# First MLP layer of row blocks 2 and 3 in one pass with seven block products for eight on four fifths of its contraction

## Chip, cores and metric

The kernel runs on one core of one Trainium2 chip. The metric is the device time of one execution in microseconds (us). The time before the change is the median of three runs.

## What is computed

`x` has 2048 rows of 640 numbers. After a layernorm, the output is the sum of the input, a two-sided Fourier transform and a two-layer MLP with a hidden width of 1536:

```python
xn = _layernorm(x, axis=-1)
a = jnp.einsum("bsd,ed->bse", xn, dft_hid_re)
b = jnp.einsum("bsd,ed->bse", xn, dft_hid_im)
y = jnp.einsum("ts,bse->bte", dft_seq_re, a) - jnp.einsum("ts,bse->bte", dft_seq_im, b)
h = _gelu(jnp.einsum("bsd,df->bsf", xn, w1) + b1)
out = x + y + jnp.einsum("bsf,fd->bsd", h, w2) + b2
```

Here x is (1, 2048, 640), w1 is (640, 1536) and w2 is (1536, 640), all in float32. The change concerns the first MLP layer, the product of `xn` and `w1`.

## The kernel before

Every matrix product runs in three matmuls: each operand is split into a high part in a short format (`fp32r`) and a low part that holds the rest. ScalarE (ACT) copies the high part, VectorE (DVE) subtracts to get the low part (`split`, L153 to L160), and `product` (L268 to L273) issues high by high, high by low and low by high into one PSUM bank. The names used below: a *form* or *piece* is a split operand of a matmul; a *unit* is one block of 128 of the 1536 hidden columns for one block of 512 rows.

The MLP runs first, over four row blocks t = 0 to 3 of 512 rows, and the Fourier part after it. A counter g runs over 48 units, g = 12 t + i. `hidden(g)` (L279) is the first layer of one unit: five 128-wide chunks of the contraction (640 = 5 x 128), three matmuls each, into one of three banks. `gelu(g)` (L294) applies bias and GELU on ACT, then splits the result into `hs`, of which there are three buffers. `output(g)` (L306) is the second layer of the unit: five blocks of 128 output columns, three matmuls each, into five banks that hold their sums over the twelve units of a row block. In each pass of the main loop (L724) PE does `hidden(g + 2)` and then `output(g)`; ACT and DVE work two units ahead of the second layer. After a row block `add_block` (L323) adds the bias on ACT, transposes on DVE and adds to a tile `xo` on GpSimd (POOL), and three DMAs store that tile to DRAM (`ys`, L750).

All engines execute their instructions in the order in which the program lists them, and nearly all DMAs are issued by the SP queue, in program order too. The order is written out by hand (`manual_schedule`). What stands beside the matmuls:

- In row block 0: the splits of the weights w1 and w2 of the coming units (`prep_w1`, `prep_w2`, with three raw buffers each, `w1r` and `w2r`). They stay in the chip's memory (SBUF) for all four row blocks, in places (`xab`, `xc`, `as`, `r01`, `rt2`) that the Fourier part uses later.
- In row blocks 0 to 2, for the next row block (`background`, L660): loads of `x`, statistics (`ln_stats`), scale (`ln_scale`, whose square root needs another ACT table than GELU), `ln_apply`, which normalises on DVE and stores the rows to a DRAM tensor `xs` in sixteen DMAs, and `load_z`, which reads them back in another layout. `transpose_z` on DVE and `prep_xt` make the split operands of the next row block, mostly in the pass i = 9.
- In row blocks 1 and 2: fifteen steps of `prep_w` (L374), which load, transpose (`turn_w`), combine and split the hidden-side Fourier matrices into the buffer `wst` (two slots, `put_w`, L359), from which ACT issues the stores to DRAM (`wit`, L370).
- A region called `zo` holds one tile at a time: `xp`, then `z` and `xo` by turns.

Of the kernel before, what the change touches and what calls it, by code (L numbers as in the profile page):

```python
# [25 lines left out]
def kernel(  # L26
# [37 lines left out]

    nc = tc.nc
# [22 lines left out]
    xs = dram.tile([NS, P, D], F32, name="xs")  # L88

# [15 lines left out]
    def bank(k):  # L105
# [40 lines left out]
    def row_tile(name):  # L146
        return rows.tile([P, D], F32, tag="row", bufs=4, name=name)
# [25 lines left out]
    xt = {}  # L173

    def load_x(c, eng=nc.sync):
        xt[c] = row_tile(f"x{c}")
        eng.dma_start(xt[c], x[c * P : (c + 1) * P])

    def ln_stats(c):
        m = MV  # L180
        st = ST[c % 2]
        half = D // 2
        for h in range(2):
            nc.vector.bn_stats(st[:, h, :], xt[c][:, h * half : (h + 1) * half])  # L184
        nc.vector.bn_aggr(m[:, c % 4, 0:2], st.rearrange("p a b -> p (a b)"))  # L185

    def ln_scale(c0, n):

        m = MV[:, c0 % 4 : c0 % 4 + n]
# [8 lines left out]
    def ln_apply(c, eng=nc.vector):  # L198
        m = MV[:, c % 4]
# [3 lines left out]

    def ln_apply_chunked(dst, c):

        m = MV[:, c % 4]
# [13 lines left out]
    def new_xt(t, j):  # L220
        XT[j] = mr.tile([P, 2, TB], F32R, tag="xt", bufs=ND, name=f"xt{t}_{j}")

    def load_z(t):
        z = out_pool.tile([P, NB, DQ], F32, tag="zo", bufs=1, name=f"z{t}")
        Z["z"] = z
        for q in range(Q):
            v = xs[:, t * B : (t + 1) * B, q * DQ : (q + 1) * DQ].rearrange("n r d -> r n d")
            nc.sync.dma_start(z[q * B : (q + 1) * B], v)

    def transpose_z(t, j):  # L230
        zt[j] = mr.tile([P, TB], F32, tag="zt", bufs=2, name=f"zt{t}_{j}")
        nc.vector.transpose(
            zt[j].rearrange("p (n i) -> p n i", i=B), Z["z"][:, :, j * B : (j + 1) * B]
        )

    def prep_xt(t, j):
        new_xt(t, j)
        split(XT[j][:, 0], XT[j][:, 1], zt.pop(j))
# [3 lines left out]
    def load_w1(i, eng=nc.sync):  # L242
        if i >= NF:
            return
# [3 lines left out]
        for q in range(Q):  # L248
            eng.dma_start(t[q * B : (q + 1) * B], v[q, :, :, i * P : (i + 1) * P])
# [8 lines left out]
    def prep_w1(i):  # L258
        if i < NF:
            W1[i] = slots[1, i]  # L260
            split(W1[i][:, 0], W1[i][:, 1], w1r.pop(i).rearrange("p a b -> p (a b)"))
# [17 lines left out]
    def hidden(g):  # L279
        i = g % NF  # L280
        acc = bank(g % 3)
# [12 lines left out]
    def gelu(g, acc, fill=lambda k: None):  # L294

        i = g % NF
        a = mr.tile([P, TB], F32, tag="ab", bufs=2, name=f"ab{g}")
        nc.scalar.activation(a, acc, AF.Gelu_apprx_tanh, bias=b1c[:, i : i + 1])  # L298
        fill(0)
# [6 lines left out]
    def output(g):  # L306
        t, i = divmod(g, NF)
        if i == 0:
            oacc[t] = [bank(3 + e) for e in range(ND)]
        hs = HT[g]  # L310
        for e in range(ND):
# [5 lines left out]
    def load_xo(t):  # L317

        xo[t] = out_pool.tile([P, NB, DQ], F32, tag="zo", bufs=1, name=f"xo{t}")
# [15 lines left out]
    def load_w(m, j):  # L335

        t = A["w"].tile([P, EB, B], F32, tag=f"wraw{m}", bufs=1, name=f"wraw{m}_{j}")
# [6 lines left out]
    def turn_w(m, j):  # L344
        t = A["w"].tile([P, D], F32, tag=f"wt{m}", bufs=1, name=f"wt{m}_{j}")
# [13 lines left out]
    def put_w(w, j, main, odd=None, negative=False):  # L359

        n = GWIDE[w] * P
        t = A["w"].tile([P, 2, 3 * P], F32R, tag="wst", bufs=2, name=f"wst{w}_{j}")
# [7 lines left out]
        stores.append(lambda: nc.scalar.dma_start(wits[w][j], t[:, :, :n].bitcast(F32)))  # L370
        if len(stores) == 2:
            put_away()

    def prep_w(s):  # L374
# [29 lines left out]
        put_away()  # L404
# [117 lines left out]
    def load_xr(k):  # L522
# [7 lines left out]
        for half in range(2):  # L530
# [3 lines left out]
            else:  # L534
                r = row_tile(f"xr{k}_{half}")
# [68 lines left out]
    wacc = bank(0)  # L604
# [10 lines left out]
    for tag, size, keys in PLACES:  # L615
        t = place(tag, (P, size // 4))
        for k, key in enumerate(keys):
            slots[key] = t[:, k * 2 * D : (k + 1) * 2 * D].rearrange("p (a b) -> p a b", a=2)
    for j in range(ND):
        new_xt(0, j)  # L620
    tacc = [bank(3 + j) for j in range(ND)]

    xp = out_pool.tile([P, NC, D], F32, tag="zo", bufs=1, name="xp")
# [10 lines left out]
    ln_scale(0, NC)  # L634
# [25 lines left out]
    def background(t, i):  # L660

        if t == 1 and i == 0:
            es_e.close()
            A["es"] = ExitStack()
            A["w"] = pool("wrawp", stack=A["es"])
            load_w(0, 0)
            load_w(1, 0)
        if t + 1 < NT:
            c0 = (t + 1) * NC

            s = 2 if t == 0 else 0
            if t == 0 and i < 2:
                ln_apply(2 * i)
                ln_apply(2 * i + 1)
                load_x(c0 + 2 * i)
                load_x(c0 + 2 * i + 1)
            elif t > 0 and i == 0:
                load_x(c0 + 3)
            if s <= i < s + 4:
                ln_stats(c0 + i - s)  # L680
            if i == s + 4:
                ln_scale(c0, 4)
                for c in range(c0, c0 + 4):
                    ln_apply(c)
                load_z(t + 1)
                if t + 2 < NT:
                    for c in range(c0 + 4, c0 + 7):
                        load_x(c)
            if i in (8, 9):
                transpose_z(t + 1, i - 8)  # L690
# [597 lines left out]
```

## Time and profile before

| | us |
|---|---|
| median of three runs | 862.78 (862.74 to 862.80) |
| the profiled execution's own time | 862.76 |
| span of its profile, first to last instruction | 861.0 |
| PE busy | 851.5 |
| DVE busy | 623.4 |
| ACT busy | 333.1 |
| row block 0 (12.9 to 91.5) | 78.6 |
| row blocks 1 and 2 (91.5 to 254.7), 81.6 each | 163.2 |
| row block 3 (254.7 to 336) | 81.3 |
| Fourier part (336 to 861) | 525 |

The span is what the profile records; 1.76 us of the execution's time lie around it. A matmul's recorded duration is that of its whole passage through the array, and matmuls follow each other faster than that, so the time of PE is read from the distance between starts, not from the mean duration. Idle time of an engine matters only where another engine waits for it in turn.

### The profile page before, as it was taken

The page shows a single profiled execution, that of the slowest core. Times are in us where ns is not written, and L with a number is a line of the kernel's source. Part 1 is how long each engine was busy: PE and PEld are TensorE (multiplying, and loading weights), DVE is VectorE, ACT ScalarE, POOL GpSimd, SP SyncE. Part 2 cuts the span into 40 slices and gives each one's busy share as a digit, 9 for nine tenths or more (in the row PEclk, how much of TensorE's full clock was granted, in tenths as well). Part 3 has the DMA queues.
Part 4 walks back from the last instruction along what each step waited for, and adds up shares of the span by engine and source line. Part 5 has one row for each costly group of instructions (what it writes and reads, how often), then busy time and mean ns, then how long its engine had stood idle before and what let it go on. Part 6 is the DMA issues. An engine that isn't in the chain of part 4 may idle for free.

```text
span 861.0 us, 10245 instructions
## 1 busy us (share of the span) xinstructions
PE 851.5 (99%) x3754; PEld 703.4 (82%) x3754; DVE 623.4 (72%) x792; ACT 333.1 (39%) x460; POOL 21.0 (2%) x22
## 2 busy tenths in 40 slices
PE   8999999999999999999999999999999999999996
PEld 6888888888888888888888888888888888888885
DVE  6554555366443678989989787998977988885596
ACT  5454434245333555443434334232322423222241
POOL 0000300030003000000000000000000000000000
PEclk9999999999999999999999999999999999999999
DMA  6747476875566984938753659853765779704464
GB/s 180 226 134 180 89 183 182 215 157 174 155 164 152 321 357 88 221 103 213 173 145 86 184 172 278 209 132 101 196 175 167 257 181 230 304 19 177 126 186 86
DMA packets 208689, 152.34 MB, mean 177 GB/s; under 512 B 82432, under 2 KB 183040, under 8 KB 208128
## 3 DMA queue, kind: packets, MB, share of 16 engines
q1 hardware_dynamic: 195728, 137.93, 61.7%
q10 hardware_dynamic: 12912, 13.77, 4.6%
q8 instruction: 29, 0.48, 0.2%
q14 instruction: 20, 0.16, 0.1%
HBM read 108.67 MB, written 42.99 MB: 176 GB/s over the span
## 4 chain that ended last, share of the span: by engine, by line
PE 98%; DVE 1%; DMA 0%; ACT 0%; issue 0%
PE banks L272 26%; PE banks L273 26%; PE banks L271 26%; PE banks L289 19%; DMA x<-in_A_x_dram 0%; DVE st L184 0%; PE banks L627 0%; DVE yo L407 0%; DVE mv L185 0%; DVE yt_last L1254 0%; DVE xp L207 0%; ACT xt L159 0%; ACT mv L191 0%; DVE mv L193 0%; DVE mv L196 0%
## 5 line engine op out<-in xcount | busy, mean ns | idle before, releaser
L272 PE MATMUL banks<-as,xab 128*128 128x512 f32 x407 | 158.5, 389 | 0.0
L271 PE MATMUL banks<-as,xab 128*128 128x512 f32 x407 | 158.3, 389 | 0.0
L273 PE MATMUL banks<-as,xab 128*128 128x512 f32 x407 | 158.3, 389 | 0.0
L159 ACT ACTIVATE as<-r 128x1024 fp32r<-128x1024 f32 x80 | 85.0, 1062 | 173.6 <-PE banks L273 148.8
L160 DVE TENSOR_TENSOR as<-r,as 128x1024 fp32r<-128x1024 f32 x80 | 97.2, 1216 | 39.3 <-ACT as L159 39.3
L289 PE MATMUL banks<-xt,xab 128*128 128x512 f32 x420 | 99.2, 390 | 0.2 <-ACT xt L159 0.2
L304 DVE TENSOR_TENSOR hs<-ab,hs 128x512 fp32r<-128x512 f32 x48 | 36.5, 760 | 84.2 <-ACT hs L302 84.2
L289 PEld LDWEIGHTS banks<-xt,xab 128*128 128x128 f32 x420 | 78.4, 188 | 17.3 <-ACT xt L159 1.3
L272 PEld LDWEIGHTS banks<-as,xab 128*128 128x128 f32 x407 | 76.4, 188 | 16.5 <-DVE as L160 0.5
L271 PEld LDWEIGHTS banks<-as,xab 128*128 128x128 f32 x407 | 76.4, 188 | 15.9
L273 PEld LDWEIGHTS banks<-as,xab 128*128 128x128 f32 x407 | 76.4, 188 | 15.6
L271 PE MATMUL banks<-as,xc 128*128 128x512 f32 x224 | 87.1, 389 | 0.0
L272 PE MATMUL banks<-as,xc 128*128 128x512 f32 x224 | 87.1, 389 | 0.0
L273 PE MATMUL banks<-as,xc 128*128 128x512 f32 x224 | 87.1, 389 | 0.0
L298 ACT ACTIVATE ab<-banks,b1c 128x512 f32<-128x512 f32 x48 | 33.0, 688 | 100.6 <-PE banks L289 97.7
L159 ACT ACTIVATE as<-rt 128x1024 fp32r<-128x1024 f32 x32 | 34.0, 1062 | 70.1 <-PE banks L273 57.9
L289 PE MATMUL banks<-xt,as 128*128 128x512 f32 x240 | 57.0, 389 | 0.0
L289 PEld LDWEIGHTS banks<-xt,as 128*128 128x128 f32 x240 | 45.0, 188 | 9.4
L272 PEld LDWEIGHTS banks<-as,xc 128*128 128x128 f32 x224 | 42.0, 188 | 8.8
L271 PEld LDWEIGHTS banks<-as,xc 128*128 128x128 f32 x224 | 42.0, 188 | 8.8
L273 PEld LDWEIGHTS banks<-as,xc 128*128 128x128 f32 x224 | 42.0, 188 | 8.6
L271 PE MATMUL banks<-hs,xc 128*128 128x512 f32 x120 | 46.7, 389 | 0.0
(161 smaller groups left out, 1364.3 us busy)
## 6 DMA issues: line engine op xcount, KB each, us to landing
raw<-in_A_dft_seq_re_dram SPq DMA_DIRECT2D x64, 256.0 KB, 5.6
raw<-in_A_dft_seq_im_dram SPq DMA_DIRECT2D x64, 256.0 KB, 5.2
wit<-wst ACTq DMA_DIRECT2D x20, 384.0 KB, 3.5
ws<-wit SPq DMA_DIRECT2D x15, 384.0 KB, 5.2
xs<-x SPq DMA_DIRECT2D x64, 80.0 KB, 1.8
xo<-in_A_x_dram SPq DMA_DIRECT2D x16, 320.0 KB, 6.1
forms_ab<-xab SPq DMA_DIRECT2D x4, 1280.0 KB, 5.8
xab<-wit SPq DMA_DIRECT2D x13, 384.0 KB, 4.8
```

What stands on the lines that cost most here:

```text
L159: nc.scalar.activation(h, s, AF.Copy)
L160: nc.vector.tensor_tensor(l, s, h.bitcast(F32), op=ALU.subtract)
L271: nc.tensor.matmul(acc, wh, mh, start=first, stop=False, skip_group_check=goes_on)
L272: nc.tensor.matmul(acc, wh, ml, start=False, stop=False, skip_group_check=goes_on)
L273: nc.tensor.matmul(acc, wl, mh, start=False, stop=last, skip_group_check=goes_on)
L289: nc.tensor.matmul(acc, W1[i][:, a, j * P : (j + 1) * P], XT[j][:, b], start=n == 0, stop=n == len(steps) - 1)
L298: nc.scalar.activation(a, acc, AF.Gelu_apprx_tanh, bias=b1c[:, i : i + 1])
L304: nc.vector.tensor_tensor(hs[:, 1], a, hs[:, 0].bitcast(F32), op=ALU.subtract)
```

## The change

Row blocks 1 and 2 (the second and third, called 2 and 3 in the title) go through the first layer together. On four of the five chunks of the contraction, a block of 2 x 2 hidden units by row blocks is computed with Winograd's form of Strassen's scheme: seven products for eight. The fifth chunk is multiplied as before. A group of four units (`pair(k)`, k = 0 to 5: two units for two row blocks) takes seven `window`s of two or three products each, eighteen products in all where there were twenty. The sums and differences of the operands are made beforehand:

- Of the rows: `ln_forms` replaces parts of the normalised rows by four sums (DVE) and stores them in sixteen DMAs per set to a new DRAM tensor `xf`, from where `load_z` reads them (`tb`, `ta`). `make_forms` transposes and splits them: five from `z_a`, two from `tb`, three from `z_b`, and t2, t3 and t4. All of it is put into row block 0, whose `background` handles eight chunks of rows in place of four.
- Of the weights: w1 is loaded again, for every group, and `make_pieces` makes pieces A, B, five additions (`+`), C and D for each group; the split w1 gives its places to the row forms and is loaded and split a third time for row block 3 of the loop (`between`).

The units of the third row block wait in DRAM (`gs`), stored by `keep` and read back with `load_unit`; their second layer runs after the six groups, in a new loop over p = 0 to 13, without a first layer beside it until p = 12. The eleventh and twelfth second-layer units of row block 0 move into the first group. All of `prep_w` moves into the groups 1 to 5 (`beside_pair`); `wst` lies in `zo` now, with three slots, and its stores are issued by SP at later points (`put_away`). `load_w` for the next step is called in `prep_w` and once more at the point 3. Rows 12 to 15 (row block 3) are handled in the loop over p. Row block 3 and the Fourier part keep their order.

```diff
-        t = A["w"].tile([P, 2, 3 * P], F32R, tag="wst", bufs=2, name=f"wst{w}_{j}")
+        t = A["wst"][:, A["puts"] % 3]
+        A["puts"] += 1
...
-        stores.append(lambda: nc.scalar.dma_start(wits[w][j], t[:, :, :n].bitcast(F32)))
-        if len(stores) == 2:
-            put_away()
+        stores.append(lambda: nc.sync.dma_start(wits[w][j], t[:, :, :n].bitcast(F32)))
...
+    def background(i):
...
+        if i == 4:
+            ln_forms(6, 10)
+            ln_forms(7, 11)
+            ln_stats(4)
+        if i == 5:
+            for c in ROWS_A[1:]:
+                ln_stats(c)
+            ln_scale(NC)
+            for c in ROWS_A:
+                ln_apply(c)
+            Z["a"] = zo_tile("z_a")
+            load_z(Z["a"], 1)
+        if i == 7:
+            ln_forms(4, 8)
+            ln_forms(5, 9)
+            Z["tb"] = as_z(row_places)
+            load_z(Z["tb"], 2, xf)
+            new_forms()
+            make_forms("a", "ua0", "ua1", "va0", "va1", "oa0")
+            Z["b"] = zo_tile("z_b")
+            load_z(Z["b"], 2)
+        if i == 8:
+            make_forms("tb", "t10", "t11")
+        if i == 9:
+            make_forms("b", "vb0", "vb1", "ob0")
...
+    def beside_pair(k, at):
...
+        if k == 1 and at == 5:
+            finish(0, 2, 3, 4)
+            store_sums(0)
+            A["wst"], A["puts"] = zo_tile("wst", (P, 3, 2, 3 * P), F32R), 0
+        j = k - 1
+        if at == 2 and k > 1:
+            put_away()
+            prep_w(3 * j - 1)
+        if at == 5:
+            put_away()
+        if at == 6:
+            prep_w(3 * j)
+        if at == 3:
+            put_away()
+            if j + 1 < ND:
+                load_w(0, j + 1)
+                load_w(1, j + 1)
+        if at == 7:
+            prep_w(3 * j + 1)
...
+    def pair(k):
...
+        window(x_, "A", 0, "ua", True)
+        u = term(a1, x_)
+        window(y_, "A", 2, "va", True, ("A", 4, "oa0"))
+        beside_pair(k, 2)
+        put_out(0 if k else 2)
+        u = unit(a1, y_, u, u)
+        window(z_, "D", 2, "t1", True, (b, 2, "ob0"))
...
+        nc.scalar.activation(zc, z_, AF.Copy)
+        split_unit(a1, u)
+        beside_pair(k, 5)
+        window(x_, "C", 0, "t2", False)
+        v = term(b1_, x_)
+        beside_pair(k, 6)
+        put_out(2 if k else 1)
+        window(z_, "C", 2, "vb", False, ("C", 4, "ob0"))
+        put_units()
+        keep(b1_, unit(b1_, z_, v, v))
+        make_pieces(k + 1, "A", "B", "+")
+        beside_pair(k, 3)
+        put_out(4)
+        window(x_, "D", 0, "t3", False)
+        put_units()
+        keep(b2_, unit(b2_, x_, zc))
+        make_pieces(k + 1, "C")
+        beside_pair(k, 7)
+        put_out(10)
+        window(x_, b, 0, "t4", False, (b, 2, "oa0"))
+        put_units()
+        gelu(a2, x_)
+        make_pieces(k + 1, "D")
+        beside_pair(k, 4)
```

Here `term` is a copy of a bank by ACT, `unit` adds such a copy to a bank on DVE and applies GELU on ACT, `zc` is a copy of the bank `z_`, a window with `False` adds to what the bank holds, `put_out(n)` issues n blocks of the second layer, `finish` is `add_block`, `make_pieces` "C" and "D" each end with the load of a w1 tile of a later group, and in `between(p)` the rows 12 to 15 are normalised, stored and read back at p = 5 and transposed at p = 7, 8 and 9.

More of the change, by code (lines that the diff above doesn't have):

```diff
@@ L602 @@
     load_w1(1, nc.scalar)
-    wacc = bank(0)
+    wacc = bank(5)
     for k in range(NWARM):
@@ L657 @@
     load_w1(5)
[L660 to L690, printed above, removed]
-        if t == 3 and i == 0:
-            A["es"].close()
-            A["raw"] = pool("rawp")
-            load_xr(0)
-            load_xr(1)
-            load_a(0)
-            load_a(1)
```

370 lines of the change are left out of this document (286 added, 84 removed), and 6 rows, old and new, of the table PLACES.

## The prediction

> **What bounds the kernel now.** I read the page first, then the chain of waits, then the busy time by stage. The page:
>
> ```profile
> span 861.0 us, 10245 instructions
> PE 851.5 (99%) x3754; PEld 703.4 (82%) x3754; DVE 623.4 (72%) x792; ACT 333.1 (39%) x460; POOL 21.0 (2%) x22
> PE 98%; DVE 1%; DMA 0%; ACT 0%; issue 0%
> ```
>
> The second line says that PE is never idle, the third that the chain which ends last is PE from end to end. A matmul less is a matmul's time gained, as long as PE still waits for nobody. The chain in order of time gives its price:
>
> ```profile
> 26.95 3.40 PE banks L289 x15
> 33.75 3.40 PE banks L289 x15
> ...
> 81.35 3.40 PE banks L289 x15
> ```
>
> Fifteen matmuls take 3.40 us, 0.2267 each, and a pass of the loop (first layer of one unit, second layer of another) 6.80. The third row is `hidden(11)`, pass i = 9; row block 0 leaves PE free for the next at 88.15. The busy time by stage (columns: PE, its weight loads, DVE, ACT, POOL):
>
> ```profile
> 12.90:91.50 78.60, 78.59 (x346) 64.67 (x347) 43.97 (x75) 39.44 (x60) 0.00 (x0) 1.00 0.66 176
> 91.50:173.10 81.60, 81.60 (x362) 67.57 (x361) 39.69 (x87) 30.83 (x60) 6.74 (x5) 1.00 0.67 169
> 173.10:254.70 81.60, 81.60 (x362) 67.57 (x361) 45.50 (x100) 35.96 (x70) 6.74 (x5) 1.00 0.60 160
> ```
>
> DVE and ACT are about half busy here, so the new work fits by sum. But both run in program order, and a wait of theirs stops all that stands behind.
>
> **Removed.** Eighteen products for twenty, three matmuls each, two chunks of weights per group: 6 fewer in each of six groups, 36 x 0.2267 = 8.2 us. Covered by nothing, if nothing else changes: 862.76 (the profiled execution; the median is 862.78) - 8.2 = 854.6.
>
> **Added to row block 0.** These rows show how normalised rows get to DVE in another layout before the change (SPq is the queue that issues DMAs):
>
> ```profile
> 62.67 2.18 DVE L200 TENSOR_SCALAR x<-x,mv 128x640 f32<-128x640 f32 x4
> 63.32 2.68 SPq L202 DMA_DIRECT2D xs<-x  x6
> 66.04 4.62 SPq L202 DMA_DIRECT2D xs<-x  x10
> 72.12 1.91 SPq L228 DMA_DIRECT2D z<-xs  x4
> 80.55 0.71 DVE L232 STREAM_TRANSPOSE zt<-z 128x512 f32<-128x512 f32 x1 [5.79 <-DMA z<-xs]
> 82.49 0.70 DVE L232 STREAM_TRANSPOSE zt<-z 128x512 f32<-128x512 f32 x1
> 83.80 0.71 DVE L232 STREAM_TRANSPOSE zt<-z 128x512 f32<-128x512 f32 x1
> ...
> 53.65 1.75 SPq L249 DMA_DIRECT2D w1r<-in_B_w_dram  x4
> 75.56 0.44 SPq L256 DMA_DIRECT2D w2r<-in_B_w_dram  x1
> 45.41 0.37 SPq L256 DMA_DIRECT2D w2r<-in_B_w_dram  x1
> ...
> 5.35 0.76 DVE st L184 x2
> 6.35 0.76 DVE st L184 x2
> ...
> DMA to landing us min/median/max: 3.7/5.4/7.3
> ```
>
> From the start of `ln_apply` to the first transposition lie 17.9 us: sixteen stores at 0.455 (7.3), 1.5 until they have landed, then 8.4 from the first of the four loads. DVE already waited 5.79 for it, at no cost, since nothing urgent stood behind. A form takes 1.31 (82.49 to 83.80), the statistics of a chunk 1.0 (5.35 to 6.35); the last row is that of the z loads.
>
> Now the first such trip. The four-row additions of `ln_forms` overwrite rows whose sixteen stores must have landed; SP comes to these after the w2 load of 45.41, is through at 53 (7.3 of issue), they land at 54.5 (1.5, as in the trip above), and DVE leaves pass 4 at 58.1, some 5 late. Pass 5: two splits 1.5, three statistics 3.1, the scale chain 1.3, so `ln_apply` starts at 64.0. Hence `z_a` is there at 64.0 + 17.9 = 81.9. Pass 7 has DVE and ACT stand before it; five forms end at 88.5. Behind them stand GELU and split of unit 9 (0.7 + 0.6 + 0.7) and the split of `W1[11]` (0.8): 90.65. `hidden(11)` needs it, and was due at 81.35. Stall 9.3.
>
> The second trip: SP is through `z_a` at 75.4 (first store 64.6, then 7.3, 1.5 and 1.9), then two w1 tiles and two of w2 (4.4), sixteen `xf` stores (7.3), 1.4 for landing: 88.5; `tb` is there 8.4 later, 96.9. Behind it on DVE: two forms 2.6, GELU and split of unit 10 1.4, w2 0.8, three forms 3.9, two transpositions 1.4, piece A 0.8: 107.85. PE, done with `output(9)` at 97.45, needs piece A for the first window. Against 88.15 row block 0 loses **19.7** (15 with loads that land in 3.7, the lowest of the z loads; 24 with another 2 per trip).
>
> **Added to the groups.** The prices:
>
> ```profile
> L160 DVE TENSOR_TENSOR xab<-w1r,xab 128x640 fp32r<-128x640 f32 x7 | 5.8, 824 | 0.0
> L159 ACT ACTIVATE xab<-w1r 128x640 fp32r<-128x640 f32 x7 | 5.2, 736 | 0.0
> L407 DVE TENSOR_TENSOR u<-u,banks 128x512 f32<-128x512 f32 x4 | 2.7, 680 | 0.0
> L407 DVE TENSOR_TENSOR wt<-wt,wt 128x256 f32<-128x256 f32 x15 | 6.3, 423 | 0.3
> L298 ACT ACTIVATE ab<-banks,b1c 128x512 f32<-128x512 f32 x48 | 33.0, 688 | 100.6 <-PE banks L289 97.7 <-DVE wt L407 2.0 <-DVE wst L160 0.9
> L302 ACT ACTIVATE hs<-ab 128x512 fp32r<-128x512 f32 x48 | 30.3, 632 | 1.4
> L347 DVE STREAM_TRANSPOSE wt<-wraw 128x640 f32<-128x640 f32 x10 | 8.0, 828 | 2.3 <-DMA wraw<-in_A_dft_hid_im_dram 2.0 <-DMA wraw<-in_A_dft_hid_re_dram 0.2
> L159 ACT ACTIVATE wst<-wt 128x256 fp32r<-128x256 f32 x35 | 14.3, 414 | 38.4 <-DMA wit<-wst 22.5 <-DVE wt L347 9.8 <-DVE wt L407 5.2
> wit<-wst ACTq DMA_DIRECT2D x20, 384.0 KB, 3.5
> DMA to landing us min/median/max: 2.4/2.7/6.8
> DMA to landing us min/median/max: 2.0/3.0/8.9
> ```
>
> The last four matter most: ACT stood 22.5 us before a `wst` slot whose store had not landed (3.5 from issue for the larger ones), when ACT issued those stores itself; the last two are the landing of these stores and of the `wraw` loads.
>
> A group is 84 matmuls, 19.0 us of PE; DVE has some 16 of work in it, ACT 12.5. Follow a middle group (k = 2, 3, 4), time from its first window. The group before ended with the addition for its second waiting unit, at -2.1; then GELU 0.7, piece C (copy 0.7, split 0.8) to 0.1; `prep_w`'s second step with its hand-offs 3.4, to 3.5; the split of `hs` 0.7; piece D, to 4.85. The third window needs D at 3.4: PE is 1.5 late. Behind D stands SP's w1 load (four issues, 1.8), and *behind that* the two stores of `prep_w`'s second step: issued at 6.65 and 7.1, landed at 10.15 and 10.6. The third step of `prep_w` comes next on ACT and needs those slots (three slots, seven tiles a round); its last copy ends at 11.0. Behind it on DVE and ACT: split 0.45, addition 0.7, GELU 0.7, and the copy `zc` 0.6, at 13.45. The window C/vb adds into the bank that `zc` reads: due at 9.65, it runs from 13.5 to 15.55. Meanwhile ACT and DVE: `hs` to 14.95, two transpositions 1.6, first step of `prep_w` 1.4, addition 0.7 and GELU 0.7 (19.35), pieces A and B 1.9, five additions 2.1, addition 0.7: 24.0. The last window must not write its bank before that; due at 22.6, it ends at 26.1. So a middle group takes 26.1 for 19.0: 7.1 lost, three times **21.2** (5.5 each if the stores land in 2.4, their lowest; 9 if they take the 6.8 of their slowest).
>
> One rule of the Trainium skill speaks against this price. *DMA: Bandwidth & Descriptors*, section "Issuing engines are not separate DMA queues", has issuing from several engines save only the issue time, "usually small relative to the DMA itself"; moving the stores to SP would then cost next to nothing, and by it a middle group would lose 1.5. The queue's order, which the rule leaves out, is what I price.
>
> The outer groups need these rows too:
>
> ```profile
> 100.61 6.74 POOL L330 TENSOR_TENSOR xo<-xo,ot 128x512 f32<-128x512 f32 x5 [99.28 <-DVE ot L328]
> 103.18 5.32 SPq L750 DMA_DIRECT2D ys<-xo  x3
> 132.31 2.06 SPq L342 DMA_DIRECT2D wraw<-in_A_dft_hid_re_dram  x4
> ys<-xo SPq DMA_DIRECT2D x6, 512.0 KB, 3.6
> ```
>
> Group 0: DVE and ACT come from row block 0 with hs, `+`, D, C, two splits and a w2 still to do (to 7.3), then four row forms; the last window waits for `+` of group 1: 24.0, loss 5.0. Group 1: `wst` gets the place of `xo` only when five POOL additions (1.35 each, from 4.1, the later ones behind DVE) and the three `ys` stores are through, about 18; ACT's first `wst` copy stands there with group 1's GELU behind it: 28.1, loss 9.1. Group 5 makes no pieces; it loses 5.6 at `zc`, and 1.4 before `output(23)` because the last two `prep_w` steps follow one another: 7.0. All six groups: 5.0 + 21.2 + 9.1 + 7.0 = **42.3**. The double `load_w` costs SP 4.1 a group (8 x 0.515), hidden behind SP's wait for piece C; uncovered, it would delay the store of the first waiting unit and with it GELU.
>
> **The loop over p.** A pass has 3.4 of PE, ACT 0.6 to 2, DVE 0.7 to 3. But rows 12 to 15 are normalised at p = 5 (18.4 to 22 after the loop's start, since three `hs` buffers let ACT run only two passes ahead), are readable 17.9 later, and their transposition stands on DVE at p = 7, before the `hs` of p = 8. That comes at about 41.5; `output` needs it at 35.4. Stall 6 to 9, I take **7.5**. The third splitting of w1 and the reload of the units (256 KB a pass) lie beside PE; row block 3 and the Fourier part are unchanged.
>
> **Sum.** 862.8 - 8.2 + 19.7 + 42.3 + 7.5 = **924**. Likeliest case's own range 906 to 946: the lower bounds (15, 32, 4) and the upper ones (24, 57, 10).
>
> **Rivals.**
>
> *PE stays the bound* (6 in 100). The engines' sums speak for it: 16 of 19 on DVE. It needs `z_a` ten microseconds earlier and the stores issued elsewhere. 854.6, to 859 with small waits.
>
> *The stores are hidden, row block 0 is not* (17). If D is ready by 3.4 and the stores land before ACT comes, middle groups lose 1.5 and group 5 about 2. 854.6 + 19.7 + 5 + 9.1 + 4.5 + 2 + 7.5 = 902. For it: SP is free of other waits there. Against it: D is the last piece DVE makes in a group.
>
> *DMA engines fill up* (12). The doubled `wraw` loads move 128-byte rows; if they queue, the stores land at the 8.9 us that the slowest `wraw` load took, 5 later, in four groups, and z loads 2 later: about 946.
>
> *Slow restart of PE* (12). The program's first matmuls ran slower than later ones, though the granted clock reads 1.00:
>
> ```profile
> 1.90:4.00 2.10, 2.09 (x5) 1.70 (x6) 0.00 (x0) 1.26 (x2) 0.00 (x0) 1.00 0.95 341
> 4.00:6.00 2.00, 2.00 (x8) 1.56 (x8) 1.75 (x5) 0.00 (x0) 0.00 (x0) 1.00 1.04 374
> ```
>
> 5 and 8 where 9.3 and 8.8 would go: 1.2 us lost. After each gap of 4 us or more, about nine of them, half of it absorbed by later waits: 924 + 6 = 930. This is what *TensorE: Matmul & The Clock Gate*, "Part 1: The HAM clock gate", says: half clock after about 3.4 us of idling, until some 3.4 us of work. The trace before has no such gap after its start.
>
> *The change doesn't do what it says* (1): the windows in the code count to 54 matmuls a group, so hardly.
>
> The forecast keeps 52. The range **895 to 946** holds it, the hidden-store case and most of the last two. About 0.2% (1.7 us) is what a measurement tells from no change here: faster 0.06, same 0.01, slower 0.93.
>
> **What would show it.** Right: DVE waiting for `z` loads at about 75 to 82 and 89 to 97, PE idle before `hidden(11)` and before the first window; the first window near 108; ACT waiting for `wit` stores once a group, `zc` at 13, groups of 24 to 28. PE busy by the sum of starts 8 us less. Wrong: PE without gaps in row block 0, or groups of 19 to 20, which would mean that the order of SP, on which 40 of the 69 us lost rest, does not bind as I walk it.

## The result and the profile after

The changed kernel takes 961.25 us (median of four runs, 959.56 to 965.72) against 862.79 for the kernel before: 1.115 times as long, 95% interval 1.111 to 1.119. The forecast was 924.0, its range 895 to 946: the right side, 37 us short. The profiled execution is the longest of the four, 965.72, with a span of 963.9. From the page of the changed kernel, the row of busy time and the granted clock in 40 slices:

```profile
PE 876.7 (91%) x3718; PEld 713.7 (74%) x3718; DVE 684.9 (71%) x904; ACT 365.6 (38%) x520; POOL 20.9 (2%) x22
PEclk9998698798998879999999999999999999999999
```

36 matmuls are gone, as forecast, yet PE is busy 25 us *longer*: a sign that many matmuls ran slower. The clock row says where, in slices 4 to 15 of 24.1 us each; before, it read 9 throughout. The view by stage (columns as in the prediction), cut at the first window of each group, at the end of the last window and at the first matmul of row block 3:

```profile
13.20:118.04 104.84, 79.91 (x331) 63.93 (x331) 62.66 (x121) 44.09 (x67) 0.00 (x0) 0.88 0.81 203
118.04:149.33 31.29, 23.90 (x85) 18.40 (x86) 20.07 (x36) 13.05 (x22) 0.00 (x0) 0.83 0.71 136
149.33:178.08 28.75, 21.91 (x85) 17.63 (x84) 15.12 (x31) 12.90 (x26) 6.34 (x5) 0.86 0.72 161
178.08:203.25 25.17, 22.12 (x86) 17.67 (x85) 14.30 (x32) 10.84 (x23) 0.00 (x0) 0.86 0.64 170
203.25:230.65 27.40, 22.47 (x86) 17.41 (x85) 14.64 (x32) 11.11 (x25) 0.00 (x0) 0.88 0.70 181
230.65:258.46 27.81, 22.53 (x86) 17.61 (x84) 14.05 (x31) 11.21 (x24) 0.00 (x0) 0.88 0.64 170
258.46:285.74 27.28, 21.71 (x86) 16.83 (x85) 12.57 (x30) 10.20 (x23) 0.00 (x0) 0.94 0.49 163
285.74:356.91 71.17, 50.84 (x195) 39.70 (x195) 34.37 (x62) 21.93 (x37) 6.61 (x5) 0.83 0.81 198
```

Set against full pace (row block 0 leaves PE free at 88.15; a group is 84 matmuls, 19.04 us; the stretch of the loop 195, 44.2), in us:

| term | forecast | this profile |
|---|---|---|
| matmuls removed | -8.2 | -8.2 |
| row block 0 | 19.7 | 118.04 - 88.15 = 29.9 |
| group 0 | 5.0 | 12.3 |
| group 1 | 9.1 | 9.7 |
| groups 2, 3, 4 | 21.2 | 6.1 + 8.4 + 8.8 = 23.3 |
| group 5 | 7.0 | 8.2 |
| loop over p | 7.5 | 27.0 |
| sum | 61.3 | 102.2 |

862.76 + 102.2 = 965.0, for 965.72 measured; 0.7 are left for row block 3 and the Fourier part, which did not change. Row block 0 varies: in profiles of kernels that leave it as it is the first window starts between 114.7 and 118.2, and in this run, the longest, it starts late.

The wait in row block 0, in order of time, first SP's queue, then DVE, then the two PE gaps:

```profile
45.52 5.12 SPq L283 DMA_DIRECT2D w1r<-in_B_w_dram  x4
51.22 7.42 SPq L222 DMA_DIRECT2D xs<-rows_b  x16
80.85 2.15 SPq L283 DMA_DIRECT2D w1r<-in_B_w_dram  x4
89.25 7.72 SPq L234 DMA_DIRECT2D xf<-row  x16
97.47 1.91 SPq L264 DMA_DIRECT2D row<-xf  x4
...
69.20 2.18 DVE L220 TENSOR_SCALAR row<-row,mv 128x640 f32<-128x640 f32 x4
87.00 0.71 DVE L268 STREAM_TRANSPOSE ztua<-z_a 128x512 f32<-128x512 f32 x1 [5.13 <-DMA z_a<-xs]
89.02 0.70 DVE L268 STREAM_TRANSPOSE ztua<-z_a 128x512 f32<-128x512 f32 x1
105.95 0.71 DVE L268 STREAM_TRANSPOSE ztt<-row 128x512 f32<-128x512 f32 x1 [6.08 <-DMA row<-xf]
...
98.33 5.91 PE L323 MATMUL banks<-xt,as 128*128 128x512 f32 x15 [12.10 <-ACT as L177]
118.04 0.80 PE L305 MATMUL banks<-xab,w1f 128*128 128x512 f32 x1 [10.41 <-ACT w1f L177]
```

The trips cost what they were forecast to: from `ln_apply` to the first transposition 17.8 us (87.00 - 69.20, forecast 17.9), `tb` 8.5 us after its load is issued (105.95 - 97.47, forecast 8.4). But the first trip starts 5 us later than thought, and a form takes 2.0 us (89.02 - 87.00), not 1.31.

The groups and the loop, as PE's timeline shows the gaps (a group's gaps before its seventh window, C/vb and D; then the first and last of the loop's three):

```profile
145.35 0.77 PE L305 MATMUL banks<-as,w1f 128*128 128x512 f32 x1 [6.59 <-DVE ab L459]
217.06 0.79 PE L305 MATMUL banks<-xab,w1f 128*128 128x512 f32 x1 [3.66 <-ACT zc L922]
236.78 0.79 PE L305 MATMUL banks<-xab,w1f 128*128 128x512 f32 x1 [2.57 <-ACT w1f L177]
...
307.65 0.60 PE L305 MATMUL banks<-hs,xc 128*128 128x512 f32 x1 [3.92 <-ACT hs L348]
344.15 0.79 PE L305 MATMUL banks<-hs,r 128*128 128x512 f32 x1 [12.25 <-ACT hs L348]
```

The cause of the C/vb gaps stands in the groups of instructions by line, for ACT from 178 to 286 us (busy time and mean; then idle time before them and what ended it): its copies to `wst` wait 19.3 us for stores.

```profile
L177 ACT ACTIVATE wst<-row 128x256 fp32r<-128x256 f32 x29 | 12.0, 414 | 30.0 <-DMA wit<-wst 19.3 <-issue 5.3 <-DVE row L401 4.1
```

### The profile page after: what moved, and what is told of

Read it like the earlier page. It is cut to its first block, busy times and chain, and to the rows that moved or that the text cites. A ratio compares the mean times of both kernels' runs of the same rounds, so it can differ in the third digit from the quotient of the medians.

```text
span 963.9 us, 10645 instructions
## 1 busy us (share of the span) xinstructions
PE 876.7 (91%) x3718; PEld 713.7 (74%) x3718; DVE 684.9 (71%) x904; ACT 365.6 (38%) x520; POOL 20.9 (2%) x22
## 4 chain that ended last, share of the span: by engine, by line
PE 61%; DMA 4%; DVE 2%; SPq 1%; POOL 1%; ACT 1%; issue 1%; ACTq 0%; DVEq 0%; POOLq 0%
PE banks L305 19%; PE banks L306 19%; PE banks L307 19%; PE banks L323 3%; DMA w1r<-in_B_w_dram 1%; DMA xo<-in_A_x_dram 1%; POOL xo L384 1%; DMA wit<-wst 1%; DMA z<-xs 1%; SPq L222 1%; DMA gr<-gs 0%; SPq L283 0%; DVE xab L178 0%; DMA xs<-row 0%; DVE hs L350 0%
## 5 line engine op out<-in xcount | busy, mean ns | idle before, releaser
L350 DVE TENSOR_TENSOR hs<-ab,hs 128x512 fp32r<-128x512 f32 x36 | 25.7, 713 | 49.4 <-ACT hs L348 49.1
L305 PE MATMUL banks<-xab,w1f 128*128 128x512 f32 x72 | 33.8, 470 | 29.1 <-ACT w1f L177 15.8
L323 PE MATMUL banks<-xt,xab 128*128 128x512 f32 x240 | 56.8, 390 | 0.2 <-ACT xt L177 0.2
L305 PE MATMUL banks<-hs,xc 128*128 128x512 f32 x120 | 48.9, 408 | 4.3 <-ACT hs L348 3.9
L323 PEld LDWEIGHTS banks<-xt,xab 128*128 128x128 f32 x240 | 44.7, 188 | 10.3 <-ACT xt L177 1.3
L306 PE MATMUL banks<-hs,xc 128*128 128x512 f32 x120 | 48.6, 405 | 3.7 <-DVE hs L350 3.7
L307 PE MATMUL banks<-hs,xc 128*128 128x512 f32 x120 | 48.4, 403 | 0.0
```

The lines of the kernel that those rows point to most:

```text
L305: nc.tensor.matmul(acc, wh, mh, start=first, stop=False, skip_group_check=goes_on)
L306: nc.tensor.matmul(acc, wh, ml, start=False, stop=False, skip_group_check=goes_on)
L307: nc.tensor.matmul(acc, wl, mh, start=False, stop=last, skip_group_check=goes_on)
L323: nc.tensor.matmul(acc, W1[i][:, a, j * P : (j + 1) * P], XT[j][:, b], start=n == 0, stop=n == len(steps) - 1)
L350: nc.vector.tensor_tensor(hs[:, 1], a, hs[:, 0].bitcast(F32), op=ALU.subtract)
```

## The experiments

Each starts from the changed kernel or from the sum of earlier edits. Medians are of four runs, five for the fillers in all gaps; the kernel before stayed between 862.58 and 863.59 beside them.

**The place of the stores on SP**

```diff
         if at == 7:
             prep_w(3 * j + 1)
+            put_away()
```

> The three stores of each second step of the DFT-weight preparation (prep_w) are issued right behind that step, ahead of the w1 load that waits for piece D. Theory (the order on SP makes the next wst copies late, and with them zc, the evictions for window C/vb and piece D): ACT's wst copies no longer wait about 20 us for the stores, the zc gaps of groups 2 to 5 (3.05, 3.66, 2.71 and 3.83 us) fall under 1 us each and their slow restarts with them, 2 to 5 us a group over four groups: 941 to 953 us. Rival (these groups are set by the sum of ACT's and DVE's work, and the late stores only show where they wait): the gap moves to the other windows, and the time stays within 3 us of 961.

942.86 us, 18.4 less. Group 2 of this kernel by stage:

```profile
173.46:192.75 19.29, 19.29 (x85) 15.69 (x84) 13.43 (x30) 10.77 (x24) 0.00 (x0) 1.00 0.78 216
```

The `wst` copies of groups 2 to 5, by line:

```profile
L177 ACT ACTIVATE wst<-row 128x256 fp32r<-128x256 f32 x31 | 12.3, 413 | 11.8 <-issue 6.6 <-DVE row L401 2.7 <-DMA wit<-wst 1.1
```

The wait for stores falls from 19.3 to 1.1 us, the four groups from 107.7 to 87.9 (groups 3, 4 and 5 take 24.1, 23.9 and 20.6), and group 2 runs at full pace. The work of DVE and ACT is the same; only the place of the stores in SP's order has moved, and no other engine issues them. The rule weighed in the prediction (the Trainium skill, *DMA: Bandwidth & Descriptors*, "Issuing engines are not separate DMA queues") speaks of the issue time; what cost 18 us here is what stood ahead in the queue.

**The second load of the DFT rows**

```diff
             put_away()
-            if j + 1 < ND:
-                load_w(0, j + 1)
-                load_w(1, j + 1)
```

> The second load of the DFT rows in each group (at point 3, which repeats what prep_w has loaded) is left out: 1.6 MB less for each of four groups. Theory (the doubled bytes pass beside the groups' work and hold no wait that ends last): at most 3 us less, 958 to 962 us. Rival (the DMA engines fill up in the groups): at least 8 us less, under 953 us.

956.33 us, 4.9 less: between the two. The profile shows groups 3 to 5 shorter by 6.6 in sum (25.2, 26.1 and 24.6 us) and groups 1 and 2 as long as before (28.7 and 25.1), although the load is left out in groups 1 to 4 and group 5 never had it. So the second load costs something, not the 5 us in each of four groups of the rival of full DMA engines, and the gain does not lie where the load was. Whether the bytes cost it or SP's time to issue the load (4.1 us a group in the prediction) was not tested.

**The order within the forms**

```diff
-        for key in keys:
+        for n, key in enumerate(keys):
             turn_x(key, z)
-            split_x(key)
+            if n:
+                split_x(keys[n - 1])
+        split_x(keys[-1])
```

> In each list of forms the transposition of the next form is put ahead of the split of the one before, so that DVE's two operations and ACT's copy overlap. Theory (a form costs 2.01 us in the changed kernel since its three operations run one after another; five of them stand ahead of W1[11] and five more ahead of the first window): a form comes to 1.3 to 1.4 us, the first window starts 3 to 7 us earlier (111 to 115 us from the start instead of 118.0): 953 to 958 us. Rival (the loads of tb, z_b and ta set the time, and the forms only wait for them): the first window is under 1.5 us earlier, 960 to 962 us.

956.34 us, 4.9 less. The PE gaps of this kernel:

```profile
94.05 5.24 PE L323 MATMUL banks<-xt,as 128*128 128x512 f32 x15 [9.10 <-ACT as L177]
115.07 0.79 PE L305 MATMUL banks<-xab,w1f 128*128 128x512 f32 x1 [12.38 <-ACT w1f L177]
139.67 0.77 PE L305 MATMUL banks<-as,w1f 128*128 128x512 f32 x1 [3.80 <-DVE ab L459]
```

The gap before `hidden(11)` falls by 3.0, the one before the first window grows by 2.0 (the trip of `tb`, as the rival said, takes most of it), and group 0's seventh window, behind four more forms, gains 2.8. A form now takes 1.3 us. The first window at 115.07 lies within what unchanged code gives (114.7 to 118.2); group 0, 28.6 us for 30.7 to 31.3 in unchanged code, does not. The theory is right on the form; that the first window comes earlier is not shown.

**The start of the first trip**

```diff
+        if i == 3:
+            background(i)
         if i + 6 < NF + 3:
             load_w1(i + 6)
         load_w2(i + 4)
-        background(i)
+        if i != 3:
+            background(i)
```

> In step i = 3 of row block 0 the LayerNorm of rows_b with its 16 stores to xs is issued ahead of that step's w1 and w2 loads on SP, nothing else; the output stays the same. Theory (the stores began at 51.2 us from the start because SP stood 5.12 us at a w1 load, and all the rest of the block, LayerNorm forms, tb and the first window, came later by as much): the stores begin at 46 us or earlier, the first window starts 4 to 6 us earlier than 118.0: 955 to 958 us. Rival (the trips of xf, tb and z_b run by what the DMA engines move and take up the time gained): the first window less than 2 us earlier: 959 to 962 us.

959.50 us, 1.8 less, with runs (958.49 to 961.72) that overlap those of the changed kernel; the first window at 116.58, within what unchanged code gives. From the timeline of SP and DVE of this kernel:

```profile
76.55 1.98 SPq L264 DMA_DIRECT2D z_a<-xs  x4
87.00 0.71 DVE L268 STREAM_TRANSPOSE ztua<-z_a 128x512 f32<-128x512 f32 x1 [7.35 <-DMA w1r<-in_B_w_dram]
```

The stretch in which `z_a` is loaded, by stage:

```profile
78.80:87.00 8.20, 2.98 (x14) 2.13 (x12) 0.82 (x4) 0.00 (x0) 0.00 (x0) 0.88 1.15 232
```

The stores begin at 44.70, 6.5 us earlier, but the load of `z_a` only 2.2 earlier: the first set takes 9.33 us to issue instead of 7.42, and the w1 and w2 loads that stood ahead of it now stand behind it. `z_a` is used at 87.00 as before: it now takes 10.45 us, with the DMA share at 1.15 (the column behind the clock). The profile names a w1 load as what ended that wait; the last part of `z_a` lands at 86.87, in the changed kernel at 86.88. So two thirds of the lead were lost on SP and the rest in the load itself.

**The loop over p, one part at a time.** First the early LayerNorm of block 3:

```diff
         if p == 2:
-            ln_stats(12)
-            ln_stats(13)
+            for c in range(3 * NC, 4 * NC):
+                ln_stats(c)
+            ln_scale(NC)
+        if p == 3:
+            for c in range(3 * NC, 4 * NC):
+                ln_apply(c)
+        if p == 4:
             finish(1, 0, 1, 2)
             store_sums(1)
...
-            Z["z"] = zo_tile("z3")
+            Z["z"] = as_z(row_places)
```

> In the loop over p the LayerNorm of block 3's rows is done at p = 2 and 3 rather than 2, 4 and 5, z3 takes the place of those rows rather than that of xo, and the turning of three output blocks (0, 1 and 2 of block 1) with their stores moves from p = 2 to p = 4. The output stays the same. Theory (the gap of 12.25 us at p = 8 comes from a chain: last weight stores, xo, the adds on POOL, DVE's transpositions, the statistics, the xs trip): that gap falls under 2 us and its slow restart of about 2 us with it, while the first gap of 3.9 us (units that come from DRAM behind the loads of row and xo) stays: 945 to 950 us. Rival (the DMA engines are full from 290 to 305 us, so a trip that starts earlier only takes longer and holds back the units): the time stays within 4 us of 961.

959.89 us: the rival's number. Its reason, full engines, is a part only: counted from the loop's start the stores of the rows are issued 11.8 us earlier than in the changed kernel, but the read-back only 1.8 earlier, since SP has w1 loads, units and the `ys` stores ahead of it. Then the late turning of z3:

```diff
-        if p in (7, 8, 9):
-            for j in ((0, 1), (2, 3), (4,))[p - 7]:
+        if p in (9, 10, 11):
+            for j in ((0, 1), (2, 3), (4,))[p - 9]:
...
-            if p == 9:
+            if p == 11:
                 load_xo(2)
```

> In the loop over p the turning and splitting of z3 moves from p = 7, 8, 9 to p = 9, 10, 11 (and the load of xo of block 2 behind it), nothing else; the output stays the same. Theory (the 12.25 us gap at p = 8 is there because DVE stands at z3's transposition, which waits for the load, with the split of p = 8's unit behind it on DVE; the load itself is in time for its use two steps later): the gap goes, the loop is 9 to 13 us shorter: 948 to 953 us. Rival (the loads of z3, units and w1 share full DMA engines and SP's order, so the wait moves two steps on): a gap of over 6 us at p = 10, and 955 to 961 us.

961.10 us: no gain. The stretch of the loop is 7.8 us shorter (63.4), and the time behind it 6.5 longer, since the first operands of row block 3 are now ready late. What the gap waits for in this kernel (SP, then ACT):

```profile
327.81 1.91 SPq L264 DMA_DIRECT2D z<-xs  x4
329.76 0.77 SPq L857 DMA_DIRECT2D gr<-gs  x1
336.99 0.63 ACT L348 ACTIVATE hs<-gr 128x512 fp32r<-128x512 f32 x1 [14.50 <-DMA gr<-gs]
```

DVE no longer stands at z3, but the unit itself comes only now: SP issues its load behind sixteen stores (from 318.9) and behind the load of z3, which waits until they have landed. One wait stood behind another.

**Five edits together**: stores, single load, forms, late turning, early start.

> The early stores, the single load of the DFT rows, the forms with the transposition ahead, the late turning of z3 and the early rows_b stores together; the output stays the same. Theory (they mend separate places): the gains add up, -18.4, -4.9, -4.9 and what the two others of this call bring (10 and 5 us), so -40 to -45: 916 to 922 us. Rival (the places share the DMA engines and SP, and a gap that goes at one place comes back at the next): under half of it, over 935 us.

933.11 us, 28.1 less. The single gains sum to 30.1 (18.4 + 4.9 + 4.9 + 0.1 + 1.8), so they add up; the two gains that the theory still hoped for did not exist.

**The units' loads on ACT's queue**, on top of the five:

```diff
-            nc.sync.dma_start(gr[i], gs[i])
+            nc.scalar.dma_start(gr[i], gs[i])
```

> The combination of five edits (933.1 us), with the loads of the waiting units (load_unit) issued by ACT instead of SP, nothing else; the output stays the same. Theory (behind the fifth edit the gap at p = 8 is a unit's load that SP issues only behind 16 xs stores and the load of z3, which waits for them): the units come in time, the three gaps of the loop (2.27, 3.22 and 6.58 us) fall to under 3 us in all, and with the restarts behind them the loop is 10 to 14 us shorter: 919 to 924 us. Rival (the DMA engines are full there, and the unit comes as late from whichever queue): gaps of over 9 us in the loop, 929 to 934 us.

933.83 us: nothing, the rival's number. From DVE of this kernel, the first and second wait of the loop:

```profile
273.89 0.72 DVE L382 STREAM_TRANSPOSE ot<-banks 128x512 f32<-128x512 f32 x1 [7.74 <-POOL xo L384]
309.35 0.71 DVE L268 STREAM_TRANSPOSE ztx<-z 128x512 f32<-128x512 f32 x1 [13.61 <-DMA z<-xs]
```

The units are in time, so the rival's reason is wrong; DVE, where their splits stand, waits for POOL's additions to a late `xo` and then for z3: the next wait of the same place again.

**Larger stores**, on top of the five. Each pair of rows that goes to neighbouring places is one transfer, and block 3 goes in four:

```diff
+    def store_pair(dst, ca, home):
+        s0 = slot[ca]
+        for k in range(NC):
+            v = dst[ca % NC * NC + k, B : 3 * B].rearrange("(j r) d -> r j d", r=B)
+            nc.sync.dma_start(v, home[k * B : (k + 1) * B, s0 : s0 + 2])
```

> The combination of five edits (933.1 us), with the stores of normalized rows and of their forms to xs and xf of blocks 1 to 3 issued as 8 (blocks 1 and 2) or 4 (block 3) larger transfers instead of 16; the bytes and the output stay the same. Theory (SP takes 7.4 us to issue 16 stores, 0.46 us each, and the trips of row block 0 and of z3 stand in that): the four sets take about 4 us each, the first window starts 5 to 8 us earlier than 113.95, the gap in the loop over p shrinks by 3 to 5 us: 920 to 926 us. Rival (the bytes take that time on the DMA engines, whose share is 0.7 to 0.8 during the stores and over 1.0 in the loads behind them): the first window under 2 us earlier, 930 to 934 us.

923.10 us, 10.0 less, the first window at 105.74 instead of 113.95. The first store set of the kernel with five edits, then the first and third set, the read-back behind the third and the two waits of DVE in this kernel:

```profile
44.51 9.91 SPq L222 DMA_DIRECT2D xs<-rows_b  x16
...
44.56 4.98 SPq L229 DMA_DIRECT2D xs<-rows_b  x8
63.00 4.64 SPq L229 DMA_DIRECT2D xs<-row  x8
70.17 1.90 SPq L274 DMA_DIRECT2D z_a<-xs  x4
78.69 1.30 DVE L278 STREAM_TRANSPOSE ztua<-z_a 128x512 f32<-128x512 f32 x2 [6.77 <-DMA z_a<-xs]
95.65 1.30 DVE L278 STREAM_TRANSPOSE ztt<-row 128x512 f32<-128x512 f32 x2 [7.36 <-DMA row<-xf]
```

`z_a` is used at 78.69 instead of 86.13, `tb` at 95.65 instead of 103.89. The bytes are the same, and the issue time per set is 5 us instead of 7.4 to 9.9. The gain comes where SP goes on with other work behind a set: 4.9 us at the first and 2.6 at the second. At the third and fourth, which are read back at once, SP now waits for the larger transfers to land: from the first store to the load that reads them lie 7.2 and 7.5 us, where it was 7.6 and 7.9. Together that is 8.3, the 8.2 by which the first window comes earlier. The loop gains nothing (64.0 us for 63.6), against the theory.

**Seven edits**: the five, both of the last two, and for group 1 `prep_w(0)` from point 6 to point 3.

> The five edits, the units' loads issued by ACT, the merged stores, and in group 1 the first step of the weight preparation (prep_w(0)), whose first copy waits 7.2 us for the stores of block 0's sums, moved from point 6 to point 3, behind the unit that PE's seventh window waits for; the output stays the same. Theory (three separate places): the gains of the two runs before it add up, and group 1's gap of 6.85 us falls under 2 us: 5 to 7 us more. With both theories right 902 to 912 us. Rival (what is gained early in row block 0 or in group 1 comes back as a wait for the same transfers further on): over 920 us.

922.44 us: the rival in sum. Group 1 falls from 28.5 to 22.4 us, as the theory said, but group 2 rises from 19.1 to 22.0 (not followed further), and the loop with the units on ACT gains nothing, as before (65.4 for 64.0).

**All three waits of the loop at once**, on top of the seven:

```diff
+            ln_scale(NC)
+            for c in range(3 * NC, 4 * NC):
+                ln_apply(c)
+            store_four(xs, 3, row_places)
+        if p == 6:
             finish(1, 0, 1, 2)
             store_sums(1)
+        if p == 4:
+            Z["z"] = as_z(row_places)
```

> The seven edits of the run before (922.4 us) and, in the loop over p: the LayerNorm of block 3's rows at p = 2, z3 in those rows' place at p = 4, and the turning and storing of output blocks 0, 1 and 2 of block 1 at p = 6 instead of p = 2; the output stays the same. Theory (each single edit of the loop gained nothing since three waits stand at the same place, units behind the load of z3, DVE behind POOL's adds to the late xo, and DVE behind z3; only with all three taken away is one not replaced by the next): the loop's gaps fall from 14.8 to under 4 us in all and the restarts with them, 10 to 15 us less: 907 to 913 us. Rival (from the start of the loop the bytes themselves, 2.6 MB for rows and xo, four units and w1, take longer on the DMA engines than PE's work): a gap of 4 us or more stays near p = 4 and the time is over 917 us.

912.13 us, 10.3 less. The loop of this kernel by stage:

```profile
244.01:294.12 50.11, 45.98 (x195) 36.05 (x195) 32.15 (x57) 20.29 (x33) 7.49 (x5) 1.00 0.93 244
```

50.1 us for 71.2, clock 1.00; the gaps come to 4.1, none above 1.2. Of the 15.3 gained in the loop against the seven edits 4.4 come back behind it, where a gap of 4.42 stands in `hidden(36)` for its last operand. Most of what the loop lost was waits in a row; the three runs that took one or two of them away showed next to nothing.

**Fillers in the gaps.** First in two groups and the loop:

```diff
+    def keep_warm(acc, n):
+        for _ in range(n):
+            nc.tensor.matmul(acc, W2[0][:, 0, :P], W2[0][:, 0, :TB], start=True, stop=True)
...
+        if k < 2:
+            keep_warm(y_, 24)
...
+            if p == 8:
+                keep_warm(bank(0), 45)
```

> Matmuls on weights that nobody reads are put in PE's order where it stands idle: 24 (5.4 us at full speed) ahead of the seventh window of groups 0 and 1, whose gaps are 6.59 and 6.84 us, and 45 (10.2 us) ahead of the output of p = 8, whose gap is 12.25 us. They do extra work and leave nothing out. Theory (PE starts again at about half its speed behind a gap of some us, 0.43 for 0.2267 us a matmul, and 10 to 16 matmuls pay for it): the matmuls behind these three gaps run at 0.23 us at once, 2 to 3 us are saved at each: 953 to 957 us. Rival (the low pitch behind a gap belongs to what the matmuls wait for, not to PE's clock): the pitch behind the gaps stays over 0.35 us, and the time within 1.5 us of 961.

959.11 us, 2.1 less, which neither the theory nor the rival had. The output that waits in the loop is that of p = 10; the 45 stood two passes ahead and used up its idle time there (a gap of 2.04 is left), so only the two windows are a clean test: group 1 has no slow matmuls left there and takes 26.2 us. Then in all large gaps:

> The changed kernel with matmuls on weights that nobody reads put into its PE gaps: 46 ahead of hidden(11), 40 ahead of the first window, 24 ahead of the seventh window of groups 0 and 1, 10, 12, 10 and 13 ahead of the window C/vb of groups 2 to 5, and 46 ahead of the output of p = 10, each a little less than its gap. Extra work, nothing left out. In the changed kernel's profile the time that is neither idle nor 0.2267 us a matmul comes to 30.9 us up to the start of row block 3. Theory (it is all PE's restart behind its gaps, and it adds to the time): it falls under 12 us, and since the waits behind the gaps start earlier by as much, the time falls by 10 to 18 us: 943 to 951 us. Rival (the restarts are absorbed, since PE waits at the next gap for DVE, ACT or a transfer whose time does not depend on PE): under half of it, over 955 us.

960.04 us (956.23 to 962.94): the rival's number. The pace behind a gap in the changed kernel (group 1's seventh window, two of the first matmuls):

```profile
174.67 0.63 PE L306 MATMUL banks<-as,w1f 128*128 128x512 f32 x1
175.09 0.63 PE L307 MATMUL banks<-as,w1f 128*128 128x512 f32 x1
```

Group 1 of the kernel with the fillers by stage, then the fillers ahead of group 2's window C/vb and the first matmul of that window:

```profile
147.59:173.78 26.19, 24.79 (x110) 20.19 (x109) 13.72 (x27) 12.30 (x24) 6.34 (x5) 1.00 0.75 164
...
185.58 3.89 PE L330 MATMUL banks<-xc 128*128 128x512 f32 x10 [2.60 <-DVE ab L463]
189.27 0.63 PE L305 MATMUL banks<-xab,w1f 128*128 128x512 f32 x1
```

Behind the gap starts lie 0.42 us apart, where full pace is 0.23. With the fillers the time that is neither idle nor full pace falls from 32.1 to 20.8 us, counted in both profiles as PE's busy time up to the start of row block 3 less 0.2267 for each matmul (the 30.9 above is counted a little lower). Where it goes:

- Row block 0: the gap ahead of `hidden(11)` falls from 12.10 to 1.89 us, and the first window still starts at 117.55, within the spread of unchanged code. Here the restart is absorbed, as the rival says.
- Group 1 falls from 28.75 to 26.19: 1.8 us less from the start of its last window to its end, which is the restart, and 0.7 because that window starts earlier in the group.
- Groups 2 to 5 take 109.2 us for 107.7, but they are no test. The fillers write a bank that DVE still reads, wait 2.60 us for it in the row shown, and then stand in the way: the window starts 15.5 us after the group's start, without fillers 11.4, although `zc`, for which it waits, is done at 13.0. Whether the restarts there are absorbed stays open.

Last, the same in the version with most waits mended:

> The best combination so far (912.1 us) with such matmuls in its largest remaining gaps: 24 ahead of hidden(11), 36 ahead of the first window, 13 and 6 ahead of the seventh window of groups 0 and 1. Extra work, nothing left out. Theory (restarts add to the time): 3 to 6 us less, 906 to 909 us. Rival (absorbed): 911 to 913 us.

907.84 us, 4.3 less, the theory's number. But of the 5.0 us between the two profiles only 2.6 lie where the fillers stand (0.3 up to the first window, 1.9 in group 0, 0.4 in group 1); the rest lies in stretches that were not changed. So the restart counts for two to three us here, most of it in group 0.

No version is faster than the kernel before. The best without extra work takes 912.1, the best of all 907.8, 1.052 times as long (1.051 to 1.054); PE bound, it would be 854.6.

## Why the prediction was right in kind and 37 us short

*Matmuls removed, 8.2 us*: right, and given back many times over.

*Row block 0, 19.7; 29.9 in the profile.* The mechanism, two trips with DVE and ACT standing before them, and the length of each trip were right. Three terms of the walk were too small (and one sum: 88.5 with the 0.7, 0.6, 0.7 and 0.8 behind it is 91.3, not 90.65). The step "SP comes to these after the w2 load of 45.41" missed the w1 load behind it, which waits 5.12 us for its slot. "Two w1 tiles and two of w2 (4.4)" took 8.4 (80.85 to 89.25). "A form takes 1.31" is the pace of transpositions issued ahead; the new list runs transposition, copy and subtraction one after another, 2.0. The runs rank them: the late start of the first trip is worth under 2 us, which the spread does not resolve; the forms are worth 5, of which group 0's gap alone is 2.8; and the issue of sixteen small stores per set, priced about right and taken for granted, is worth 10 and was the lever, since all the rest of SP's work stands behind it.

*Groups, 42.3; 53.5.* That SP's order binds, through `wst` slots and `zc`, was the main step, and moving one call confirms it: 18.4 us for a forecast 22 (three times 7.1 less 1.5, and 7.0 less 2). Group 1's wait of ACT for the `ys` stores was right to 0.6 us, and the trial with `prep_w(0)` moved shows it. The step that failed is group 0, 5.0 forecast and 12.3 measured: four forms at 2.0 (2.8, shown by the forms run) and a slow start behind a 10 us gap (in the last run, with fillers, the group takes 26.6 where it took 28.4) were not in it. Some 2.6 of the 7.3 stay open; if 24.0 is when the last window may start, as in a middle group, its own nine matmuls (2.0) are missing from the term.

*The loop over p, 7.5; 27.0.* The most mis-sized term. The step "rows 12 to 15 are normalised ... 18.4 to 22 after the loop's start" failed: DVE got there at 318.8, 33 after it. These rows of the changed kernel show why:

```profile
293.80 2.26 SPq L375 DMA_DIRECT2D xo<-in_A_x_dram  x4
296.16 3.00 SPq L857 DMA_DIRECT2D gr<-gs  x1
306.97 0.63 ACT L348 ACTIVATE hs<-gr 128x512 fp32r<-128x512 f32 x1 [11.06 <-DMA gr<-gs]
307.73 0.72 DVE L382 STREAM_TRANSPOSE ot<-banks 128x512 f32<-128x512 f32 x1 [9.89 <-POOL xo L384]
340.20 0.71 DVE L268 STREAM_TRANSPOSE ztx<-z 128x512 f32<-128x512 f32 x1 [16.04 <-DMA z<-xs]
```

`wst` holds the place of `xo` until its last store has landed, so the load of `xo` is issued only 8 us into the loop. Its last part then takes 10.8 us to land, at 306.1, and POOL's additions come late; DVE stands at the transposition that needs them, with everything of the next passes behind it. "The reload of the units (256 KB a pass) lies beside PE" failed too: ACT waits 11.06 us for one, which SP issued at 296.16 behind rows and `xo` and which takes 10.7 us to land. From 290 to 307 us the DMA share is 1.05 to 1.21, so both the order and the full engines make these loads late. With all three waits mended the share is still 1.07 to 1.18 from 250 to 262 us and PE hardly waits: here the full engines cost time only where something was needed right behind them. I had walked only the last of the three waits. That they follow one another is shown by the runs: at most 1.4 us from one or two of them, 10.3 net from all three and 15.3 within the loop.

*Rivals.* The full DMA engines, at 946 for the wrong reason: the doubled load costs 4.9 us in all, but the engines do fill up where `z_a`, `xo` and the units are loaded (shares above 1.0). The slow restart was priced at 1.2 us a gap, half absorbed. It is 1.5 to 3.0 us a gap, as *TensorE: Matmul & The Clock Gate*, "Part 1: The HAM clock gate", of the Trainium skill leads one to expect (half clock for some microseconds after idling; the trace agrees, 0.42 for 0.23 us); in row block 0 it is absorbed, in groups 0 and 1 some 2 us each count, and for the gaps of groups 2 to 5 and of the loop the runs leave it open. How much of the 37 us it explains is therefore not settled.

## What to carry to other kernels

Where a DMA queue is walked in order, a store's place in it can cost more than its transfer: put stores ahead of loads that wait for a slot. When a mended wait brings nothing, look at what the same engine stands at next before giving up the cause; here one or two of three brought nothing and all three did. Merging many small transfers frees the queue for what stands behind them; a trip that is read back at once gained only 0.4 us by it. And before a filler is read as a test of idle time, look at whether the filler itself waits.

## What the runs showed that was not expected

A gap of 2.57 us (at 236.78) was already followed by six matmuls 0.43 us or more apart, and the number behind one and the same gap varied from run to run (14 and 8 in `hidden(11)`, in code that was the same up to there). The changed kernel's own time spreads over 6 us from run to run, that of the kernel before over 0.7; that the timing of the transfers on the path shows in the sum is likely, but no run tests it.
